# Attention streamed from HBM on one core: TensorE's program touches its far end first and ends with a wait for the last store, and the last V buffer is freed in two parts

## The chip, the core and the metric

The kernel runs on one core of a Trainium2 chip. The metric is device time in microseconds (us) of one execution; lower is better. All times of the trace are counted from the first instruction of the profiled execution.

## What is computed

```python
B, H, Sq, Skv, Dh = 8, 16, 16, 2048, 256          # q, k, v in bfloat16
scale = q.shape[-1] ** -0.5
scores = jnp.einsum('bhqd,bhkd->bhqk', q, k) * scale
attn = jax.nn.softmax(scores, axis=-1)
return jnp.einsum('bhqk,bhkd->bhqd', attn, v)
```

There are 128 heads, each with 16 queries and 2048 keys. K and V are 134 MB each, and every byte of them is read once, so the work is mostly a stream of two large tensors through the core.

## The kernel before

**Stages.** The 128 heads are worked off in 16 stages g = 0..15 of eight heads. A stage needs K and V of its eight heads, each in two halves of four heads; the code calls the half e = 0 or 1, and this document says K(g,a), K(g,b), V(g,a), V(g,b). A half is 4 MB: 128 partitions with 64 tokens (T) of 256 numbers each. `SL` has four buffers of that size, KA, KB, VA and VB. K of stage 0 goes into VA and VB; all later K goes into KA and KB, all V into VA and VB.

**SyncE** issues every load (`load`, L93, its DMA on L94) and the last store, in one fixed order (`on_sync`, L96): q, K(0,a), K(0,b), then for g = 1..15 K(g,a), K(g,b), V(g-1,a), V(g-1,b), and V(15,a), V(15,b) at the end. A load waits until the buffer that it overwrites has been read: K(g,e) waits for `c_qk[e]` (L103), which TensorE raises when it has used up K(g-1,e); V(w,e) waits for `c_pv[e]` (L115), raised when V(w-1,e) has been used up; V(0,e) waits for `c_qk[e]` of stage 0. SyncE waits at the head of its queue, so a load that waits holds back all loads behind it. Near the end loads are cut into pieces: K(15,a) and K(15,b) into two of 32 tokens, V(14,b) into 33 and 31 tokens, V(15,a) into 37 and 27 and V(15,b) into eight pieces from 19 down to 2 tokens (`PIECES`, L83, and `MID`, L85). Each piece has a semaphore of its own, so that TensorE can start on the first ones.

**VectorE** transposes each half of K in place in two instructions of 32 tokens each (L145), raising `c_kt[e][0]` and `c_kt[e][1]`. Later in the stage it takes the negative row maximum (L147), transposes the probabilities into `PTc` (L153) and inverts the row sums.

**ScalarE** prepares the scaled queries of the next stage (L165), takes the exponential (L191, raising `c_ex`), and spreads the transposed probabilities into the block pattern `PTz` by eight copies (L180, each raising `c_cp`): four for half a, after `c_pv[0]` says that half a of `PTz` is free, then the evacuation of the stage before (L173, raising `c_ev`) with its store, then four for half b.

**TensorE** (`on_tensor`) first runs QK for stage 0. Then follows a loop over r = 1..16 in TensorE's own program (a real loop with a branch back, not unrolled): QK of stage r (left out for r = 16), then PV of stage r-1. `qk` (L217, by way of `mm`) issues eight weight loads with one matmul of 128x512 for each bank c in `cs` behind each load (L212 is the matmul with a load, L213 those without). In the loop it is called four times, twice for each half, with two of the four banks at a time: banks 0 and 1 need only the first 32 tokens, so the first call waits for `c_kt[e][0]` and the second for `c_kt[e][1]`. QK for half a also waits for `c_ex[1]`, since it overwrites the scores of the stage before. PV is 64 matmuls of 128x256 for each half (L251), one for each token t, all into one bank; it waits for `c_ev`, for the copies (`c_cp`), for the V half (`s_v`) and in front of the first token of each piece for that piece (`s_p`).

**The end.** After PV of stage 15 ScalarE evacuates the result, SyncE stores it (L126, 64 KB) and waits for that store (`s_fin`, L127). TensorE's program ends when its loop ends, without a wait.

Of the kernel before, what the change touches and what calls it, by code (L numbers as in the profile page):

```python
# [4 lines left out]
ACTF = mybir.ActivationFunctionType  # L5
# [6 lines left out]
T = 64  # L12
# [3 lines left out]
def bass_standalone__softmax_full_bidir__sampling_kernel(  # L16
# [20 lines left out]
    with ExitStack() as es:  # L37
# [17 lines left out]
        def sem(name):  # L55
            return ec(nc.semaphore(name))
# [13 lines left out]
        c_ex = [sem("c_ex0"), sem("c_ex1")]  # L70
        c_pt = sem("c_pt")
        c_ri = sem("c_ri")
        c_cp = sem("c_cp")
        c_pv = [sem("c_pv0"), sem("c_pv1")]
        c_ev = sem("c_ev")

# [13 lines left out]
        def kslot(g, e):  # L90
            return (VA, VB)[e] if g == 0 else (KA, KB)[e]
# [4 lines left out]
        def on_sync(eng):  # L96
            eng.dma_start(QT[:], qh).then_inc(s_q, 16)  # L97
            for e in range(2):
                load(eng, ku, 0, e, kslot(0, e), 0, T, s_k0[e])
            for g in range(1, G):  # L100
                for e in range(2):
                    if g >= 2:
                        eng.wait_ge(c_qk[e], g)  # L103
                    if g < last:
                        load(eng, ku, g, e, kslot(g, e), 0, T, s_k[e])
                    else:
                        load(eng, ku, g, e, kslot(g, e), 0, 32, s_k[e])
                        load(eng, ku, g, e, kslot(g, e), 32, 32, s_kl[e])
                if g == 1:
                    for x in [c_ev] + list(s_p[0].values()) + list(s_p[1].values()):  # L110
                        eng.sem_inc(x, 1)
                for w in ((g - 1,) if g < last else (g - 1, g)):
                    for e in range(2):
                        if w:
                            eng.wait_ge(c_pv[e], w)  # L115
                        else:
                            eng.wait_ge(c_qk[e], 1)
                        pieces = [(0, T)]
                        if w == last:
                            pieces = PIECES[e]  # L120
                        elif (w, e) == (last - 1, 1):
                            pieces = [(0, MID), (MID, T - MID)]
                        for a, n in pieces:
                            load(eng, vu, w, e, (VA, VB)[e], a, n, s_p[e][a] if a else s_v[e])
            eng.wait_ge(c_ev, G + 1)
            eng.dma_start(oh[128 * last:128 * last + 128, :], O_fin[:, last, :]).then_inc(s_fin, 16)  # L126
            eng.wait_ge(s_fin, 16)  # L127
# [4 lines left out]
        def on_vector(eng):  # L132
            eng.memset(QW[:].rearrange("p e m x -> p (e m x)").bitcast(F32), 0.0).then_inc(c_qt, 1)  # L133
            eng.wait_ge(s_q, 16)
            qf = QT[:].bitcast(F32)
            eng.transpose(qf, qf).then_inc(c_qt, 1)  # L136
            for g in range(G):
                for e in range(2):
                    for h in range(2):
                        if h == 0:  # L140
                            eng.wait_ge(s_k[e] if g else s_k0[e], 16 * max(g, 1))
                        elif g == last:
                            eng.wait_ge(s_kl[e], 16)
                        x = SLf[:, kslot(g, e), 32 * h:32 * h + 32, :].rearrange("p t i -> p (t i)")
                        eng.transpose(x, x).then_inc(c_kt[e][h], 1)  # L145
                eng.wait_ge(c_qk[1], g + 1)
                eng.tensor_reduce(out=negm[:, g:g + 1], in_=S_ps[:].rearrange("p c n -> p (c n)"),  # L147
                                  axis=AX.X, op=ALU.max, negate=True).then_inc(c_mx, 1)
                for h in range(2):
                    eng.wait_ge(c_ex[h], g + 1)  # L150
                    if g and h == 0:
                        eng.wait_ge(c_cp, 8 * g)
                    eng.transpose(PTc[:, 32 * h:32 * h + 32, :].rearrange("p t x -> p (t x)"),  # L153
                                  P_sb[:, 1024 * h:1024 * h + 1024]).then_inc(c_pt, 1)
                eng.tensor_reduce(out=ltot[:, g:g + 1], in_=lsum[:, g, :], axis=AX.X, op=ALU.add).then_inc(c_ri, 1)  # L155
                eng.wait_ge(c_ri, 2 * g + 1)
                eng.reciprocal(rinv[:, g:g + 1], ltot[:, g:g + 1]).then_inc(c_ri, 1)  # L157

        def on_scalar(eng):
            def qwb(g):  # L160
                Q, r = g // 4, g % 4
                for a in range(4):
                    dv = QW[32 * a:32 * a + 32, 0, 16 * a, :]
                    sv = QT[32 * Q:32 * Q + 32, :]
                    eng.activation(ap_of(dv, dv.offset, [[1024 + 512, 2], [2, 64], [1, 2]]),  # L165
                                   ap_of(sv, sv.offset + 2 * (8 * r + a), [[8, 2], [64, 64], [1, 2]]),
                                   ACTF.Copy, scale=scale).then_inc(c_qw, 1)

            def evac(g):
                eng.wait_ge(c_pv[1], g + 1)  # L170
                if g == last:
                    eng.wait_ge(c_ri, 2 * G)
                eng.activation(O_fin[:, g, :], O_ps[:, 0:D], ACTF.Copy, scale=rinv[:, g:g + 1]).then_inc(c_ev, 1)  # L173

            def copies(e):
                for a in range(4):
                    rs = 32 * (2 * e + a // 2)
                    sv = PTc[rs:rs + 32, :, :]
                    m = 64 * e + 16 * a
                    eng.activation(PTz[32 * a:32 * a + 32, e, :, m:m + 16],  # L180
                                   sv[:, :, 16 * (a % 2):16 * (a % 2) + 16], ACTF.Copy).then_inc(c_cp, 1)

            eng.wait_ge(c_qt, 2)
            qwb(0)
            for g in range(G):
                if g < last:
                    eng.wait_ge(c_qk[1], g + 1)
                    qwb(g + 1)
                eng.wait_ge(c_mx, g + 1)
                for h in range(2):  # L190
                    eng.activation(P_sb[:, 1024 * h:1024 * h + 1024],  # L191
                                   S_ps[:, 2 * h:2 * h + 2, :].rearrange("p c n -> p (c n)"), ACTF.Exp,
                                   bias=negm[:, g:g + 1], scale=1.0, accum_out=lsum[:, g, h:h + 1]).then_inc(c_ex[h], 1)
# [12 lines left out]
            eng.wait_ge(s_st, 16 * last)  # L206

        def on_tensor(eng):
# [18 lines left out]
            eng.wait_ge(c_qw, 4)  # L227
            for e in range(2):
                eng.wait_ge(c_kt[e][1], 1)
                qk(e, (0, 1, 2, 3), kslot(0, e)).then_inc(c_qk[e], 1)  # L230

            with nc.Fori(1, G + 1, engines=[PE]) as r:
                with eng.If_lt(eng.to_reg(r), G):
                    for e in range(2):
                        for h in range(2):
                            eng.wait_ge(c_kt[e][h], r + 1)
                            if e == 0 and h == 0:
                                eng.wait_ge(c_ex[1], r)
                            ins = qk(e, (2 * h, 2 * h + 1), (KA, KB)[e])
                        ins.then_inc(c_qk[e], 1)  # L240
                lim1 = (r & 16) + 1
                lim2 = lim1 + ((r + 1) & 16)
                for e in range(2):
                    if e == 0:
                        eng.wait_ge(c_ev, r)
                    eng.wait_ge(c_cp, 8 * r - 4 + 4 * e)
                    eng.wait_ge(s_v[e], 16 * r)
                    for t in range(T):
                        if t in s_p[e]:
                            eng.wait_ge(s_p[e][t], lim2 if (e, t) == (1, MID) else lim1)  # L250
                        ins = eng.matmul(O_ps[:, 0:D], PTz[:, e, t, :], SL[:, (VA, VB)[e], t, :],  # L251
                                         start=(e == 0 and t == 0), stop=(e == 1 and t == T - 1))
                    ins.then_inc(c_pv[e], 1)

        on_sync(nc.sync)
        on_gpsimd(nc.gpsimd)
# [31 lines left out]
```

## Time and profile before

| | |
|---|---|
| three timed runs | 638.52, 637.37 and 638.66 us, median 638.52 |
| the profiled execution's own time | 637.77 us |
| its span, first to last instruction | 636.4 us |
| TensorE busy with matmuls, VectorE, ScalarE | 77%, 57%, 33% of the span |
| matmuls and weight loads | 3072 and 2544 |
| mean granted TensorE clock | 0.921 of full speed |
| bytes read by DMA | 269.48 MB |

The profiled execution's time is the span and 1.4 us around it. The profile's page has a row of 40 equal slices for each engine, in tenths of busy time; DMA in that row is the mean busy share of the 16 DMA engines, and the row below it is what they moved. "SPq" and "PEq" are the queues of SyncE and TensorE. A row of the timeline has the start, the length, the engine, the line and operation, how many such instructions were merged ("x2"), and in brackets the idle time ahead of it with what ended that. A row of the DMA issues ends with the time from issue to the last landing; a 4 MB load is one issue, and 16 DMA engines carry an equal part each.

### The profile page before, as it was taken

To read this page: it belongs to the slowest core of one execution; us is meant where nothing else is said; L and a number is where in the kernel's file an instruction comes from. 1 tells how busy PE (TensorE), PEld (TensorE's weight loads), DVE (VectorE), ACT (ScalarE), POOL (GpSimd) and SP (SyncE) were. 2 spreads that over 40 slices of the span, in tenths; PEclk is the share of its full clock that TensorE was granted. 3 is DMA by queue.
4 is the path that set the end of the run, shared out by engine and by line. 5 is a ranking of instruction groups with operands and counts; after the bars stand their busy time and mean duration, and the time that the engine had idled before them with its cause. 6 is when DMAs were issued, how large, how long until landed. Compare 5 with 4: busy or idle time off the path is not lost.

```text
span 636.4 us, 6411 instructions
## 1 busy us (share of the span) xinstructions
PE 489.3 (77%) x3072; PEld 271.0 (43%) x2544; DVE 361.7 (57%) x146; ACT 207.4 (33%) x273; POOL 7.1 (1%) x5
## 2 busy tenths in 40 slices
PE   0457999595995958879597895967959589597787
PEld 0002737154271533716336262452714428154376
DVE  2949683763738546294562935639366383766610
ACT  1024535225052250613416043160522505225050
POOL 4000000000000000000000000000000000000000
PEclk9997999798897989979799797998979899799999
DMA  8999999999999999999999999999999999999997
GB/s 371 445 437 420 413 432 430 431 432 434 433 430 432 431 431 432 439 432 430 430 431 428 432 432 431 435 431 432 428 432 435 430 433 437 426 427 425 431 395 288
DMA packets 13254, 270.60 MB, mean 425 GB/s; under 512 B 1472, under 2 KB 3776, under 8 KB 4416
## 3 DMA queue, kind: packets, MB, share of 16 engines
q1 hardware_dynamic: 11088, 269.55, 98.7%
q10 hardware_dynamic: 2160, 0.98, 0.5%
q8 instruction: 2, 0.03, 0.0%
q14 instruction: 4, 0.03, 0.0%
HBM read 269.48 MB, written 1.05 MB: 425 GB/s over the span
## 4 chain that ended last, share of the span: by engine, by line
DMA 63%; DVE 23%; PE 13%; ACT 0%; issue 0%; SPq 0%
DMA SL<-in_k_dram 56%; DVE SL L145 22%; DMA SL<-in_v_dram 7%; PE S_ps L213 5%; PE S_ps L212 5%; PE O_ps L251 4%; DVE PTc L153 0%; DVE negm L147 0%; ACT P_sb L191 0%; SPq L94 0%; ACT O_fin L173 0%; SPq L97 0%; DVE rinv L157 0%; DVE ltot L155 0%
## 5 line engine op out<-in xcount | busy, mean ns | idle before, releaser
L145 DVE STREAM_TRANSPOSE SL<-SL 128x4096 f32<-128x4096 f32 x64 | 280.8, 4424 | 154.8 <-DMA SL<-in_k_dram 154.8
L212 PE MATMUL S_ps<-SL,QW 128*128 128x512 bf16 x496 | 206.6, 417 | 140.3 <-DVE SL L145 140.2
L251 PE MATMUL O_ps<-SL,PTz 128*128 128x256 bf16 x2048 | 228.6, 273 | 3.4 <-DMA SL<-in_v_dram 3.2
L251 PEld LDWEIGHTS O_ps<-SL,PTz 128*128 128x128 bf16 x2048 | 198.4, 98 | 37.2 <-issue 7.5
L213 PE MATMUL S_ps<-SL,QW 128*128 128x512 bf16 x528 | 213.2, 414 | 0.0
L212 PEld LDWEIGHTS S_ps<-SL,QW 128*128 128x128 bf16 x496 | 72.6, 146 | 324.5 <-issue 177.7
L180 ACT ACTIVATE PTz<-PTc 32x1024 bf16<-32x1024 bf16 x128 | 134.9, 1054 | 48.3 <-PE O_ps L251 38.0
L165 ACT ACTIVATE QW<-QT 32x256 bf16<-32x256 bf16 x64 | 26.8, 419 | 297.8 <-PE S_ps L213 290.7
L147 DVE TENSOR_REDUCE negm<-S_ps 128x1 f32<-128x2048 f32 x16 | 36.7, 2292 | 64.9 <-PE S_ps L213 64.9
L153 DVE STREAM_TRANSPOSE PTc<-P_sb 128x1024 bf16<-128x1024 bf16 x32 | 37.9, 1224 | 20.3 <-ACT P_sb L191 20.3
L191 ACT ACTIVATE P_sb<-S_ps,negm 128x1024 bf16<-128x1024 f32 x32 | 35.4, 1110 | 26.5 <-DVE negm L147 26.5
L173 ACT ACTIVATE O_fin<-O_ps,rinv 128x256 bf16<-128x256 f32 x16 | 7.6, 474 | 52.8 <-PE O_ps L251 52.8
L130 POOL MEMSET PTz<- 128x8192 f32 x1 | 6.9, 6925 | 0.3 <-POOLq L273 0.3
L191 ACT ACTIVATION_READ_ACCUMULATOR P_sb<-S_ps,negm 128x1 f32 x32 | 6.3, 196 | 0.0
L136 DVE STREAM_TRANSPOSE QT<-QT 128x2048 f32<-128x2048 f32 x1 | 2.3, 2311 | 3.7 <-DMA QT<-in_q_dram 3.7
L157 DVE RECIPROCAL rinv<-ltot 128x1 f32<-128x1 f32 x16 | 2.6, 164 | 0.5
L155 DVE TENSOR_REDUCE ltot<-lsum 128x1 f32<-128x2 f32 x16 | 1.8, 113 | 0.0
L165 ACT ACT_TABLE_LOAD x1 | 1.3, 1283 | 0.7 <-PEq L273 0.7
L133 DVE MEMSET QW<- 128x1024 f32 x1 | 0.9, 912 | 1.0 <-PEq L273 1.0
L273 POOL MEMSET const-bfloat16-1.0<- 128x1 bf16 x1 | 0.1, 103 | 0.0
L273 POOL MEMSET const-uint8-127<- 128x1 uint8 x1 | 0.1, 103 | 0.0
L273 POOL MEMSET const-float32-0.0<- 128x1 f32 x1 | 0.1, 100 | 0.2 <-issue 0.2
(1 smaller groups left out, 0.1 us busy)
## 6 DMA issues: line engine op xcount, KB each, us to landing
SL<-in_k_dram SPq DMA_DIRECT2D x30, 4096.0 KB, 25.8
SL<-in_v_dram SPq DMA_DIRECT2D x29, 4096.0 KB, 29.1
SL<-in_k_dram SPq DMA_DIRECT2D x4, 2048.0 KB, 23.0
SL<-in_v_dram SPq DMA_DIRECT2D x1, 2368.0 KB, 8.6
SL<-in_v_dram SPq DMA_DIRECT2D x1, 2112.0 KB, 27.2
SL<-in_v_dram SPq DMA_DIRECT2D x1, 1984.0 KB, 31.5
SL<-in_v_dram SPq DMA_DIRECT2D x1, 1728.0 KB, 12.5
SL<-in_v_dram SPq DMA_DIRECT2D x1, 1216.0 KB, 8.9
```

The costliest lines, as they stand in the source:

```text
L130: eng.memset(PTz[:].rearrange("p a t c -> p (a t c)").bitcast(F32), 0.0).then_inc(c_pool, 1)
L145: eng.transpose(x, x).then_inc(c_kt[e][h], 1)
L147: eng.tensor_reduce(out=negm[:, g:g + 1], in_=S_ps[:].rearrange("p c n -> p (c n)"), axis=AX.X, op=ALU.max, negate=True).then_inc(c_mx, 1)
L153: eng.transpose(PTc[:, 32 * h:32 * h + 32, :].rearrange("p t x -> p (t x)"), P_sb[:, 1024 * h:1024 * h + 1024]).then_inc(c_pt, 1)
L157: eng.reciprocal(rinv[:, g:g + 1], ltot[:, g:g + 1]).then_inc(c_ri, 1)
L165: eng.activation(ap_of(dv, dv.offset, [[1024 + 512, 2], [2, 64], [1, 2]]), ap_of(sv, sv.offset + 2 * (8 * r + a), [[8, 2], [64, 64], [1, 2]]),
L173: eng.activation(O_fin[:, g, :], O_ps[:, 0:D], ACTF.Copy, scale=rinv[:, g:g + 1]).then_inc(c_ev, 1)
L180: eng.activation(PTz[32 * a:32 * a + 32, e, :, m:m + 16], sv[:, :, 16 * (a % 2):16 * (a % 2) + 16], ACTF.Copy).then_inc(c_cp, 1)
L191: eng.activation(P_sb[:, 1024 * h:1024 * h + 1024], S_ps[:, 2 * h:2 * h + 2, :].rearrange("p c n -> p (c n)"), ACTF.Exp, bias=negm[:, g:g ...
L212: return eng.matmul(dst, w, x, start=start, stop=stop)
L213: return eng.add_instruction(mybir.InstMatmult(name=nc.get_next_instruction_name(), engine=PE, start_tensor_calc=start, stop_tensor_calc=stop,
L251: ins = eng.matmul(O_ps[:, 0:D], PTz[:, e, t, :], SL[:, (VA, VB)[e], t, :], start=(e == 0 and t == 0), stop=(e == 1 and t == T - 1))
```

## The change

- TensorE's program is put into named blocks. It starts with a branch to a block "far", which stands behind the loop's end and does nothing but branch back to "near", the program proper. After the loop TensorE branches to "over", behind "far".
- In "over" TensorE waits for the last store (`s_fin`), as SyncE does.
- PV of half a raises a new semaphore `c_pm` after token 36. SyncE issues the first 37 tokens of V(15,a) after `c_pm` of the 15th pass, and the other 27 after `c_pv[0]`, as before.
- In the loop, QK for half a is one call with all four banks (one weight load for four matmuls, eight loads instead of 16), and waits for the whole transposed half, `c_kt[0][1]`. Half b stays at two calls.
- `c_cp` becomes two semaphores, one for each half of `PTz`; VectorE waits for both.
- The limits for the waits are computed into registers at other places of the loop.

```diff
-        c_cp = sem("c_cp")
+        c_cp = [sem("c_cp0"), sem("c_cp1")]
+        c_pm = sem("c_pm")
...
                         if w:
-                            eng.wait_ge(c_pv[e], w)
+                            eng.wait_ge(c_pm if (w, e) == (last, 0) else c_pv[e], w)
...
                         for a, n in pieces:
+                            if (w, e, a) == (last, 0, PIECES[0][1][0]):
+                                eng.wait_ge(c_pv[0], w)
                             load(eng, vu, w, e, (VA, VB)[e], a, n, s_p[e][a] if a else s_v[e])
...
                     if g and h == 0:
-                        eng.wait_ge(c_cp, 8 * g)
+                        for x in c_cp:
+                            eng.wait_ge(x, 4 * g)
...
-            with nc.Fori(1, G + 1, engines=[PE]) as r:
-                with eng.If_lt(eng.to_reg(r), G):
+            nc.br("far", engines=[PE])
+            with nc.body("near", valid_engines=[PE]):
...
+                with nc.Fori(1, G + 1, engines=[PE]) as r:
+                    rr = eng.to_reg(r)
+                    r4, r16, lim1 = eng.to_reg(4 * r), eng.to_reg(16 * r), eng.to_reg((r & 16) + 1)
+                    with eng.If_lt(rr, G):
+                        for e in range(2):
+                            for cs in (((0, 1, 2, 3),), ((0, 1), (2, 3)))[e]:
+                                eng.wait_ge(c_kt[e][cs[-1] // 2], r + 1)
+                                if e == 0:
+                                    eng.wait_ge(c_ex[1], rr)
+                                ins = qk(e, cs, (KA, KB)[e])
+                            ins.then_inc(c_qk[e], 1)
                     for e in range(2):
-                        for h in range(2):
-                            eng.wait_ge(c_kt[e][h], r + 1)
-                            if e == 0 and h == 0:
-                                eng.wait_ge(c_ex[1], r)
-                            ins = qk(e, (2 * h, 2 * h + 1), (KA, KB)[e])
-                        ins.then_inc(c_qk[e], 1)
...
+                        for t in range(T):
...
+                            if (e, t + 1) == (0, PIECES[0][1][0]):
+                                ins.then_inc(c_pm, 1)
+                        ins.then_inc(c_pv[e], 1)
+                        if e == 0:
+                            lim2 = eng.to_reg((r & 16) + ((r + 1) & 16) + 1)
+                nc.br("over", engines=[PE])
+            with nc.body("far", valid_engines=[PE]):
+                eng.nop()
+                nc.br("near", engines=[PE])
+            nc.switch_bb("over")
+
+            eng.wait_ge(s_fin, 16)
```

More of the change, by code (lines that the diff above doesn't have):

```diff
@@ L180, in copies @@
                     eng.activation(PTz[32 * a:32 * a + 32, e, :, m:m + 16],
[L181 removed]
+                                   sv[:, :, 16 * (a % 2):16 * (a % 2) + 16], ACTF.Copy).then_inc(c_cp[e], 1)
             eng.wait_ge(c_qt, 2)
@@ L225, in qk @@
                 return ins
[L227 to L230, printed above, removed]
-            with nc.Fori(1, G + 1, engines=[PE]) as r:
-                with eng.If_lt(eng.to_reg(r), G):
-                    for e in range(2):
-                        for h in range(2):
-                            eng.wait_ge(c_kt[e][h], r + 1)
-                            if e == 0 and h == 0:
-                                eng.wait_ge(c_ex[1], r)
-                            ins = qk(e, (2 * h, 2 * h + 1), (KA, KB)[e])
-                        ins.then_inc(c_qk[e], 1)
[L241 to L253, printed above, removed]
@@ new lines, in on_tensor @@
+            nc.br("far", engines=[PE])
+            with nc.body("near", valid_engines=[PE]):
+                eng.wait_ge(c_qw, 4)
+                for e in range(2):
+                    eng.wait_ge(c_kt[e][1], 1)
+                    qk(e, (0, 1, 2, 3), kslot(0, e)).then_inc(c_qk[e], 1)
+                with nc.Fori(1, G + 1, engines=[PE]) as r:
+                    rr = eng.to_reg(r)
+                    r4, r16, lim1 = eng.to_reg(4 * r), eng.to_reg(16 * r), eng.to_reg((r & 16) + 1)
+                    with eng.If_lt(rr, G):
+                        for e in range(2):
+                            for cs in (((0, 1, 2, 3),), ((0, 1), (2, 3)))[e]:
[4 more added lines that the diff above has]
+                            ins.then_inc(c_qk[e], 1)
+                    for e in range(2):
+                        if e == 0:
+                            eng.wait_ge(c_ev, rr)
+                        eng.wait_ge(c_cp[e], r4)
+                        eng.wait_ge(s_v[e], r16)
+                        for t in range(T):
+                            if t in s_p[e]:
+                                eng.wait_ge(s_p[e][t], lim2 if (e, t) == (1, MID) else lim1)
+                            ins = eng.matmul(O_ps[:, 0:D], PTz[:, e, t, :], SL[:, (VA, VB)[e], t, :],
+                                             start=(e == 0 and t == 0), stop=(e == 1 and t == T - 1))
+                            if (e, t + 1) == (0, PIECES[0][1][0]):
+                                ins.then_inc(c_pm, 1)
+                        ins.then_inc(c_pv[e], 1)
+                        if e == 0:
+                            lim2 = eng.to_reg((r & 16) + ((r + 1) & 16) + 1)
+                nc.br("over", engines=[PE])
```

## The prediction, made before the changed kernel was run

> **What bounds the kernel now.** I read the page's span, slices and chain first.
>
> ```profile
> span 636.4 us, 6411 instructions
> DMA  8999999999999999999999999999999999999997
> HBM read 269.48 MB, written 1.05 MB: 425 GB/s over the span
> DMA 63%; DVE 23%; PE 13%; ACT 0%; issue 0%; SPq 0%
> ```
>
> The DMA engines are full in every slice but the first and the last. The chain's DVE and PE parts are work that releases loads while earlier loads still run. So the end moves only by time in which the DMA engines are left without work, and by what follows the last landing. In the middle a late issue costs nothing:
>
> ```profile
> SL<-in_k_dram SPq DMA_DIRECT2D x30, 4096.0 KB, 25.8
> SL<-in_v_dram SPq DMA_DIRECT2D x29, 4096.0 KB, 29.1
> ```
>
> A K half lands 25.8 us after its issue. Its own transfer takes 9.7 us: in the rows below V(0,a) lands at 33.05 + 21.1 = 54.2 and V(0,b) at 41.09 + 22.8 = 63.9. So it stood behind other loads for some 16 us. I then looked for the places without such cover, by landing times and the windows, and found two, and a third thing behind the last landing.
>
> **Place 1, the load of K(2,a).** Timeline and DMA issues, stages 0 and 1:
>
> ```profile
> 24.22 0.62 PE L212 MATMUL S_ps<-SL,QW 128*128 128x512 bf16 x1 [24.22 <-DVE SL L145]
> 33.05 0.33 SPq L94 DMA_DIRECT2D SL<-in_v_dram  x1
> 41.09 0.33 SPq L94 DMA_DIRECT2D SL<-in_v_dram  x1
> 47.18 8.75 DVE L145 STREAM_TRANSPOSE SL<-SL 128x4096 f32<-128x4096 f32 x2
> 51.66 0.65 PE L212 MATMUL S_ps<-SL,QW 128*128 128x512 bf16 x1 [10.61 <-DVE SL L145]
> 60.49 8.25 SPq L94 DMA_DIRECT2D SL<-in_k_dram  x2
> ...
> SL<-in_v_dram SPq DMA_DIRECT2D x1, 4096.0 KB, 21.1
> SL<-in_v_dram SPq DMA_DIRECT2D x1, 4096.0 KB, 22.8
> SL<-in_k_dram SPq DMA_DIRECT2D x1, 4096.0 KB, 15.1
> 68.42 16.84 DMA SL<-in_k_dram
> ```
>
> K(2,a) is issued at 60.49, when QK(1,a) has ended, only 3.4 us ahead of V(0,b)'s landing at 63.9, and everything behind it in SyncE's queue waits too. It lands at 75.6, 11.7 us after V(0,b) where 9.7 would do: 2.0 us are lost already. K(2,b) follows at 85.3, 9.7 later, and from there on the queue is deep.
>
> **Place 2, the load of V(15,a).**
>
> ```profile
> 580.15 0.80 SPq L94 DMA_DIRECT2D SL<-in_v_dram  x2
> 602.32 7.17 PE O_ps L251 x64
> 609.51 0.33 SPq L94
> 616.50 0.47 ACT L173 ACTIVATE O_fin<-O_ps,rinv 128x256 bf16<-128x256 f32 x1 [2.63 <-PE O_ps L251]
> ...
> SL<-in_v_dram SPq DMA_DIRECT2D x1, 1984.0 KB, 31.5
> SL<-in_v_dram SPq DMA_DIRECT2D x1, 2368.0 KB, 8.6
> 609.00:610.00 1.00, 1.00 (x12) 0.90 (x10) 0.00 (x0) 0.43 (x1) 0.00 (x0) 1.00 0.63 270
> 610.00:611.00 1.00, 1.00 (x12) 0.90 (x10) 0.00 (x0) 0.98 (x2) 0.00 (x0) 1.00 1.39 370
> 611.00:612.00 1.00, 1.00 (x12) 0.90 (x10) 0.00 (x0) 0.98 (x2) 0.00 (x0) 1.00 0.44 152
> 612.00:616.00 4.00, 4.00 (x39) 3.59 (x38) 0.00 (x0) 1.84 (x2) 0.00 (x0) 1.00 1.03 433
> ```
>
> V(15,a) is issued at 609.51, when PV(14,a) has ended; the last piece of V(14,b), the second issue behind 580.15, lands 31.5 us after it, at 612.0. The last column, GB/s, falls to 270, 370 and 152 in three windows and is 433 afterwards: (270 + 370 + 152)/433 = 1.8 of 3 us were used, 1.2 lost. By the last landings it is less: the first piece (37 of 64 tokens, 5.6 us of transfer) lands at 618.1, 6.1 after 612.0: 0.5 lost.
>
> **The end.**
>
> ```profile
> q8 instruction: 2, 0.03, 0.0%
> ...
> q8 instruction: 1, 0.02, 5.8%
> ...
> DMA packets 145, 0.08 MB, mean 33 GB/s; under 512 B 16, under 2 KB 144, under 8 KB 144
> q8 instruction: 1, 0.02, 3.4%
> ...
> q1 hardware_dynamic: 9, 0.00, 2.7%
> ...
> 633.59 0.35 SPq L126 DMA_DIRECT2D out_dram<-O_fin  x1
> SPq L127 <- DMA out_dram<-O_fin: 2.5, 1, 2.5
> ```
>
> In the window 634.0 to 636.45 one packet of the instruction queue ran for 3.4% of 16 engines' 2.45 us, 1.3 us, beside the 144 packets of the last store. In the window 635.2 to 636.45 nine of those 144 are left, one engine's sixteenth. So fifteen engines were done by 635.2, and one, behind the code fetch, at the span's end, 636.4: the fetch holds the store up by 1.2 us. The other packet of this queue (the second row, window 68 to 69) ran when TensorE entered the second part of its loop for the first time; I take the queue for TensorE's.
>
> **The change part by part**, against the profiled execution's own 637.77 us (span 636.4 and 1.4 around it); the median shown, 638.52, is 0.75 above it.
>
> *QK for half a in one call.* 15 x 8 = 120 weight loads go. They lie beside matmuls: stage 0, with one load for four matmuls, takes 24.22 to 33.05 = 8.83 us for 32, stage 1, with one for two, 51.66 to 60.49 = 8.83. Worth nothing. But QK(1,a) now starts when both transposes are done, 47.18 + 8.75 = 55.93, not at 51.66, and takes at least the same 8.83 us. K(2,a) is then issued at 64.8 or later, after V(0,b) has landed. How much later hangs on the granted clock, the column ahead of the last two:
>
> ```profile
> 51.60:54.90 3.30, 3.24 (x8) 0.79 (x5) 3.30 (x2) 3.23 (x4) 0.00 (x0) 0.50 1.06 457
> 158.00:164.10 6.10, 6.02 (x15) 1.27 (x8) 5.00 (x3) 0.00 (x0) 0.00 (x0) 0.50 1.02 437
> ```
>
> After an idle stretch QK starts at half the clock, here for 3.3 us in stage 1 and for 6.1 in a later one. At half clock a matmul takes 3.3/8 = 0.41 us, at full 0.22, so each further us costs half a us: up to 1.4. K(2,a) is issued at 64.8 to 66.2. An empty queue starts with a delay: V(15,a)'s first piece landed 8.6 us after its issue for 5.6 of transfer, 3.0 on top. K(2,a) lands at 64.8 + 3.0 + 9.7 = 77.5 to 78.9 instead of 75.6: +2.0 to +3.4. I take the middle, **+2.7**. From the other side: the engines' mean rather than the last landing could put it at 4.0; the start of the kernel, where q is issued at 0.74 and K(0,b) has landed at 25.0 with 2.4 + 2 x 9.7 us of transfer, had a delay of 2.4 and would give +1.3. Nothing behind it can give that back, as the queue is full until place 2.
>
> In stages 2 to 14 the same delay, 4 to 5 us at QK(g,a) and less at PV, lies inside the 16 us of cover: nothing. Without that cover it would cost 4 us a stage. In stage 15 K(15,a)'s second transpose releases QK at 587.15; 64 matmuls at 0.22 end at 601.2, and V(14,a) lands at 602.3: 1.1 us of room, which a half clock would use up. The rows, with those of the start and the end:
>
> ```profile
> 587.15 0.44 PE L212 MATMUL S_ps<-SL,QW 128*128 128x512 bf16 x1 [1.16 <-DVE SL L145]
> ...
> 573.01 29.26 DMA SL<-in_v_dram
> ...
> 633.09 0.47 ACT O_fin L173
> ...
> 0.74 0.38 SPq L97
> 1.65 23.35 DMA SL<-in_k_dram
> ```
>
> *The last V in two parts.* `c_pm` rises after 37 of PV(14,a)'s 64 matmuls, 602.32 + 37 x 0.11 = 606.4, 3.1 us ahead of 609.51. SyncE has nothing else between; the second piece follows at 609.5 as before, and V(15,b), behind it, waits for 616.5 anyway. 5.6 us of lead should nearly close the gap; place 1 lost some with 3.4. Gain 0.5 to 1.2, taken **-0.9**. TensorE is next: PV(15) is 128 matmuls at 7.17/64 = 0.11 us, 14.3 in all, and can start at 617.0, when the evacuation of stage 14 is done, ending at 631.3. The evacuation after it now starts at 633.09, so 1.8 us of room are left.
>
> *The far branch and the end wait.* The branch out and back runs while TensorE idles up to 24.22. It moves the fetch near 69 us to the start, where it delays one of 16 engines; place 1 levels that: nothing. [...] The store then lands at 635.2: **-1.2**, bounds 0 and -1.3.
>
> [...]
>
> *The rest.* `c_cp` in two semaphores: the copies run in order on ScalarE, so the same copies release the same waits. The register work is a few instructions beside 7 us of matmuls. Nothing.
>
> **The sum**: 637.8 + 2.7 - 0.9 - 1.2 = **638.4 us**, 0.1 under the median.
>
> **Rivals.**
> 1. *The start is hidden* (faster). If the queue of V(0,b) is deeper than I read, or the half clock shorter, K(2,a) costs at most 1 us: 637.8 + 0.7 - 0.9 - 1.2 = 636.4. For it: the rows show one execution. Against: 64.8 is after 63.9.
> 2. *The long clock* (slower). 6.1 us of half clock at QK(1,a), and half clock again at QK(15,a), which takes the gain of place 2: 637.8 + 3.4 + 0 - 1.2 = 640.0. It decides once the stretch in stage 1 passes 5 us. For it: other stages show it. Against: by the delay above TensorE idles only some 4 us ahead of QK(15,a), against 10.6 ahead of QK(1,a).
> [...]
> 4. *The wait does not keep the fetch away*: 637.8 + 2.7 - 0.9 = 639.6, within the bound.
>
> **How the numbers follow.** A measurement tells about 0.2%, 1.3 us, from no change. Forecast 0.40 and rival 4 0.08 lie within it: 0.48 the same. Rival 1 has 0.22: faster. Rivals 2 and 3 have 0.12 and 0.18: slower 0.30. The range has to take in most of rivals 1 and 3: 636.2 to 640.8; the forecast's own is 637.2 to 639.6.
>
> **What would show it.** K(2,a) issued at 65 to 66 and landing at 77.5 to 79, GB/s near zero in a window ahead of it: step one. V(15,a)'s first piece issued 5 to 6 us ahead of V(14,b)'s last landing, and no window under 400 GB/s there: step two. No instruction packet beside the last store, all its packets landed within 1.6 us of the issue, and the span ending there: step three. The forecast is wrong if K(2,a) lands at 76, or if the time around the span grows by the fetch.

## The result

The changed kernel is slower: 641.58 us in the median of five runs (640.84 to 641.72), beside 638.47 for the kernel before on the same chip (five runs, 637.13 to 638.66). The ratio is 1.0052, with a 95% interval of 1.0037 to 1.0067. That is above the forecast of 638.4 and above the range's upper end of 640.8. The profiled execution took 641.72 us, 3.95 more than that of before: its span is 640.0 instead of 636.4, and around the span lie 1.7 us instead of 1.4.

The page of the changed kernel, its span, slices, instruction queue, traffic and the share of the chain (in the numbering of its own lines, L148 is the K transpose, L216 and L217 are QK, L258 is PV, L95 the loads):

```profile
span 640.0 us, 6279 instructions
DMA  8999899999999999999999999999999999999997
GB/s 372 442 430 395 328 428 430 436 443 432 430 426 432 429 433 440 436 430 426 427 431 432 432 442 435 428 426 430 426 433 441 440 430 426 430 424 427 433 419 280
q8 instruction: 1, 0.02, 0.0%
HBM read 269.48 MB, written 1.05 MB: 423 GB/s over the span
DMA 48%; PE 28%; DVE 23%; ACT 0%; issue 0%; SPq 0%
```

The slices show where to look. All of them are as full as before except the fifth, 64 to 80 us, with 328 GB/s, and a little less in the one ahead of it. This is place 1.

**Place 1.** The timeline of the changed kernel, stages 0 and 1, and K(2,a)'s issue row (the last column is the time from issue to landing):

```profile
16.83 4.45 DVE L148 STREAM_TRANSPOSE SL<-SL 128x4096 f32<-128x4096 f32 x1 [7.40 <-DMA SL<-in_k_dram]
25.75 0.62 PE L216 MATMUL S_ps<-SL,QW 128*128 128x512 bf16 x1 [25.75 <-DVE SL L148]
48.71 17.40 DVE L148 STREAM_TRANSPOSE SL<-SL 128x4096 f32<-128x4096 f32 x4
57.52 0.65 PE L216 MATMUL S_ps<-SL,QW 128*128 128x512 bf16 x1 [14.93 <-DVE SL L148]
66.56 0.33 SPq L95 DMA_DIRECT2D SL<-in_k_dram  x1
...
SL<-in_k_dram SPq DMA_DIRECT2D x1, 4096.0 KB, 12.1
```

QK(1,a) starts at 57.52 behind two transposes, 48.71 + 8.8, as the prediction said, but everything here is 1.5 us later than it reckoned: QK(0) starts at 25.75 and not at 24.22. K(2,a) is issued at 66.56 and lands at 78.7. The windows of the changed kernel (columns as in the prediction, the last is GB/s), and behind them two of before:

```profile
62.00:63.00 1.00, 1.00 (x6) 0.15 (x1) 1.00 (x1) 0.00 (x0) 0.00 (x0) 1.00 0.76 328
63.00:64.00 1.00, 1.00 (x7) 0.14 (x1) 1.00 (x1) 0.00 (x0) 0.00 (x0) 1.00 0.08 33
64.00:65.00 1.00, 1.00 (x6) 0.14 (x1) 1.00 (x1) 0.00 (x0) 0.00 (x0) 1.00 0.00 0
65.00:66.00 1.00, 1.00 (x7) 0.14 (x1) 1.00 (x1) 0.00 (x0) 0.00 (x0) 1.00 0.00 0
66.00:67.00 1.00, 1.00 (x6) 0.28 (x2) 0.12 (x1) 0.00 (x0) 0.00 (x0) 1.00 0.00 0
67.00:68.00 1.00, 1.00 (x6) 0.37 (x3) 0.00 (x0) 0.00 (x0) 0.00 (x0) 1.00 1.84 492
```

```profile
63.00:64.00 1.00, 1.00 (x5) 0.14 (x1) 1.00 (x1) 0.00 (x0) 0.00 (x0) 1.00 1.08 361
64.00:65.00 1.00, 0.42 (x3) 0.22 (x2) 0.58 (x1) 0.00 (x0) 0.00 (x0) 1.00 1.05 360
```

From 63 to 67 us the DMA engines of the changed kernel move almost nothing: four microseconds in which the stream that sets the time stands still. Before, the same place shows two windows of 360.

**Place 2.** The changed kernel around the last V (the rows of QK(15) are in the first two lines, with the granted clock ahead of the last two columns):

```profile
590.40:597.20 6.80, 5.75 (x14) 0.63 (x4) 5.75 (x3) 1.12 (x2) 0.00 (x0) 0.50 1.04 443
597.20:604.00 6.80, 6.80 (x33) 1.60 (x11) 4.12 (x1) 0.00 (x0) 0.00 (x0) 1.00 1.03 443
616.00:622.00 6.00, 6.00 (x58) 5.38 (x56) 0.00 (x0) 3.77 (x4) 0.00 (x0) 1.00 0.96 411
622.00:625.00 3.00, 2.43 (x24) 1.94 (x22) 0.00 (x0) 2.08 (x3) 0.00 (x0) 1.00 0.95 358
625.00:626.00 1.00, 1.00 (x12) 0.90 (x10) 0.00 (x0) 0.97 (x2) 0.00 (x0) 1.00 0.68 236
626.00:627.00 1.00, 1.00 (x12) 0.90 (x10) 0.00 (x0) 0.97 (x2) 0.00 (x0) 1.00 1.01 374
627.00:628.00 1.00, 1.00 (x12) 0.89 (x10) 0.00 (x0) 0.66 (x1) 0.00 (x0) 1.00 0.91 370
```

The gap ahead of V(15,a) is closed (411 GB/s from 616 to 622), but a new one stands behind it: against 415 GB/s the windows from 622 to 628 lose (3 x 57 + 179 + 41 + 45)/415 = 1.05 us. V(15,b) waits for the end of PV(14), and PV(14) is late: TensorE idled for 5.1 us ahead of QK(15) and then ran at half clock for 6.8 us, so that PV(14) starts at 608.3, 1.7 us after V(14,a) has landed (606.6). What the early piece of V(15,a) gained went back there.

**The end.** The store in the changed kernel:

```profile
637.90 0.47 ACT L177 ACTIVATE O_fin<-O_ps,rinv 128x256 bf16<-128x256 f32 x1 [10.24 <-PE O_ps L258]
638.40 0.35 SPq L129 DMA_DIRECT2D out_dram<-O_fin  x1
...
out_dram<-O_fin SPq DMA_DIRECT2D x1, 64.0 KB, 1.5
```

No instruction packet, and 1.5 us instead of 2.8. The evacuation starts 4.8 us later than before (637.90 against 633.09), the store gives 1.3 back, and 0.3 to 0.4 come behind the span: 4.8 - 1.3 + 0.4 = 3.9, the difference of the two profiled executions.

### The profile page after: what moved, and what is told of

Read it like the earlier page. It is cut to its first block, busy times and chain, and to the rows that moved or that the text cites. A ratio compares the mean times of both kernels' runs of the same rounds, so it can differ in the third digit from the quotient of the medians.

```text
span 640.0 us, 6279 instructions
## 1 busy us (share of the span) xinstructions
PE 483.0 (75%) x3072; PEld 254.3 (40%) x2424; DVE 361.6 (57%) x146; ACT 207.4 (32%) x273; POOL 7.1 (1%) x5
## 3 DMA queue, kind: packets, MB, share of 16 engines
HBM read 269.48 MB, written 1.05 MB: 423 GB/s over the span
## 4 chain that ended last, share of the span: by engine, by line
DMA 48%; PE 28%; DVE 23%; ACT 0%; issue 0%; SPq 0%
DMA SL<-in_k_dram 47%; DVE SL L148 21%; PE S_ps L217 17%; PE S_ps L216 7%; PE O_ps L258 3%; DMA SL<-in_v_dram 1%; DVE PTc L157 1%; DVE negm L150 1%; ACT P_sb L195 0%; SPq L95 0%; ACT O_fin L177 0%; SPq L98 0%; DVE rinv L161 0%; DVE ltot L159 0%
## 5 line engine op out<-in xcount | busy, mean ns | idle before, releaser
L148 DVE STREAM_TRANSPOSE SL<-SL 128x4096 f32<-128x4096 f32 x64 | 280.8, 4424 | 121.1 <-DMA SL<-in_k_dram 121.1
L216 PE MATMUL S_ps<-SL,QW 128*128 128x512 bf16 x376 | 152.8, 406 | 154.1 <-DVE SL L148 154.0
L258 PE MATMUL O_ps<-SL,PTz 128*128 128x256 bf16 x2048 | 226.7, 273 | 0.8 <-ACT O_fin L177 0.6
L217 PE MATMUL S_ps<-SL,QW 128*128 128x512 bf16 x648 | 226.5, 421 | 0.0
L258 PEld LDWEIGHTS O_ps<-SL,PTz 128*128 128x128 bf16 x2048 | 199.5, 98 | 31.3 <-issue 4.9
L216 PEld LDWEIGHTS S_ps<-SL,QW 128*128 128x128 bf16 x376 | 54.7, 146 | 352.0 <-issue 217.5
```

Source lines behind the costliest of these rows:

```text
L216: return eng.matmul(dst, w, x, start=start, stop=stop)
L217: return eng.add_instruction(mybir.InstMatmult(name=nc.get_next_instruction_name(), engine=PE, start_tensor_calc=start, stop_tensor_calc=stop,
```

## The experiments

The theory from these two traces: place 1 is the loss. The merged call starts QK(1,a) late, and the far branch, which the prediction costed at nothing, makes it later. The rivals: the far branch alone; the late QK in every stage; something at the end. Each kernel ran beside the kernel before on the same chip, whose median was 637.02 in the first group, 636.89 in the second and 636.90 in the third, so ratios are compared, not times.

| kernel | median us | ratio to before, 95% interval |
|---|---|---|
| the whole change (five runs with the prediction) | 641.58 | 1.0052 [1.0037, 1.0067] |
| e1 changed, without the far branch | 640.15 | 1.0048 [1.0029, 1.0067] |
| e2 changed, QK half a in two calls | 636.93 | 1.0000 [0.9989, 1.0010] |
| e3 before, merged call alone | 641.52 | 1.0069 [1.0050, 1.0088] |
| e4 before, end wait alone | 637.45 | 1.0006 [0.9994, 1.0017] |
| e5 before, V(15,a) in two parts alone | 636.54 | 0.9988 [0.9976, 1.0000] |
| e6 before, far branch alone | 638.17 | 1.0009 [0.9997, 1.0020] |
| e7 before, two parts and end wait | 636.62 | 0.9995 [0.9984, 1.0006] |
| e9 changed, K(1,a) transposed early | 635.77 | 0.9979 [0.9969, 0.9989] |
| e8 before, two parts, end wait, K(1,a) half early | 635.87 | 0.9982 [0.9971, 0.9994] |
| e10 before, two parts, K(1,a) early | 635.46 | 0.9981 [0.9971, 0.9990] |
| e11 the whole change again | 640.79 | 1.0061 [1.0047, 1.0075] |
| e12 as e1, beside e11 | 639.87 | 1.0048 [1.0031, 1.0064] |

### The merged call: e3, e2

e3 is the kernel before with QK of half a in one call:

```diff
-                        for h in range(2):
-                            eng.wait_ge(c_kt[e][h], r + 1)
-                            if e == 0 and h == 0:
+                        for cs in (((0, 1, 2, 3),), ((0, 1), (2, 3)))[e]:
+                            eng.wait_ge(c_kt[e][cs[-1] // 2], r + 1)
+                            if e == 0:
                                 eng.wait_ge(c_ex[1], r)
-                            ins = qk(e, (2 * h, 2 * h + 1), (KA, KB)[e])
+                            ins = qk(e, cs, (KA, KB)[e])
```

> The kernel before with one edit: QK of half a in one call that waits for both transposes. Theory: QK(1,a) starts at 55.9, K(2,a) is issued at 64.8 to 66.2 and lands at 77.5 to 79; time 640.5 to 642.0, as slow as the whole change, since the store still ends behind the fetch. Rival, the merged call is hidden: 637.5 to 638.7.

It took 641.52 us, ratio 1.0069: this edit alone is at least as slow as the whole change. Place 1 of e3, timeline, issue row and windows:

```profile
56.19 0.65 PE L212 MATMUL S_ps<-SL,QW 128*128 128x512 bf16 x1 [14.93 <-DVE SL L145]
65.44 0.33 SPq L94 DMA_DIRECT2D SL<-in_k_dram  x1
...
SL<-in_k_dram SPq DMA_DIRECT2D x1, 4096.0 KB, 13.4
...
64.00:65.00 1.00, 1.00 (x6) 0.14 (x1) 0.78 (x1) 0.00 (x0) 0.00 (x0) 1.00 0.00 0
65.00:66.00 1.00, 1.00 (x6) 0.38 (x3) 0.00 (x0) 0.00 (x0) 0.00 (x0) 1.00 0.00 0
```

K(2,a) is issued at 65.4 and lands at 78.8, in the expected bounds. It also shows the second cost of the merged call. PV(14) starts at 607.36 and V(15,a) is issued at 614.54, 5.0 us later than before, where place 1 explains 3.3: QK(15) ran at half clock from 589.5 to 596.2 (0.50 in that window), and in this kernel V(15,a) waits for all of PV(14,a). In landings, K(2,a) comes 3.3 us later than before (78.8 against 75.6), and so does the last piece of V(14,b) (615.3 against 612.0); the first piece of V(15,a) comes 4.9 later (614.54 + 8.5 = 623.0 against 618.1). So in this execution some 3.3 us were lost at place 1 and 1.6 at place 2.

e2 is the changed kernel with the call split again:

```diff
-                            for cs in (((0, 1, 2, 3),), ((0, 1), (2, 3)))[e]:
+                            for cs in ((0, 1), (2, 3)):
```

> The changed kernel with QK of half a in two calls again, as half b has it (eight weight loads more in the loop). Theory: QK(1,a) starts with the first transposed 32 tokens near 53.1, K(2,a) is issued at 62 to 63.5 and lands at 75 to 77; QK(15) is done before V(14,a) lands, so the early part of V(15,a) keeps its gain; time 636.3 to 638.0. Rival, the merged call costs nothing and the branch at the start is the loss: K(2,a) is late all the same and the time stays above 640. Also told: whether the wait for the store still keeps the code fetch away from it when the program is eight instructions longer.

636.93, ratio 1.0000: undoing this one edit takes the whole loss away, K(2,a) is issued at 61.95, and there is no gain left over, though both edits that were to gain are in. Both halves of the pair say the same, so the merged call as the main cause is shown, not only argued.

### Is it place 1, or the late QK of every stage: e9

e9 is the whole change, and VectorE transposes both parts of K(1,a) before the softmax of stage 0; K(1,a) has landed by then and VectorE is idle:

```diff
+            EARLY = [(1, 0, 0), (1, 0, 1)]
...
             for g in range(G):
                 for e in range(2):
                     for h in range(2):
+                        if (g, e, h) not in EARLY:
+                            kt(g, e, h)
+                if g == 0:
+                    for x in EARLY:
+                        kt(*x)
```

(`kt` holds the wait and the transpose that stood in the loop.)

> The whole change, and VectorE transposes K(1,a), which landed at 35 us, before the softmax of stage 0 instead of behind it. Nothing else moves, the merged call and the far branch stay. Theory, place 1 is the bulk of the loss: QK(1,a) starts near 48 to 50 instead of 57.5, K(2,a) is issued at 57 to 60 and lands at 74 to 76 instead of 78.7; 3.5 to 4.3 us under the changed kernel, ratio to the kernel before 0.998 to 1.001. Rival, the late QK of every stage and the fetch are the loss: ratio 1.003 or more.

635.77, ratio 0.9979: with the merged call in all 15 stages, the far branch and the end wait still in, the kernel is faster than before. Its rows at place 1, the transpose, the issue and two windows:

```profile
35.91 8.77 DVE L148 STREAM_TRANSPOSE SL<-SL 128x4096 f32<-128x4096 f32 x2 [0.94 <-DMA SL<-in_k_dram]
58.12 0.33 SPq L95 DMA_DIRECT2D SL<-in_k_dram  x1
...
63.00:64.00 1.00, 1.00 (x6) 0.40 (x3) 0.00 (x0) 0.00 (x0) 0.00 (x0) 1.00 1.07 459
64.00:65.00 1.00, 1.00 (x7) 0.29 (x4) 0.00 (x0) 0.00 (x0) 0.00 (x0) 1.00 1.22 524
```

K(2,a) is issued some 7 us before V(0,b) has landed (42.26 + 22.8 = 65.1), and nothing is lost. From 1.0052 to 1.0061 for the change to 0.9979 is some 0.8%, 5 us, by one move on an engine that is idle there, and more than the 3.5 to 4.3 us that were expected, since place 1 now loses less than in the kernel before. Place 1 is the cause. The late QK of stages 2 to 14 costs nothing that can be told, as predicted: e10 below, with K(1,a) early and without the merged call, the branch and the wait, has 0.9981.

### The far branch: e1, e12 beside e11, e6

e1 and e12 are the changed kernel without the two branches:

```diff
-            nc.br("far", engines=[PE])
-            with nc.body("near", valid_engines=[PE]):
...
-                nc.br("over", engines=[PE])
-            with nc.body("far", valid_engines=[PE]):
-                eng.nop()
-                nc.br("near", engines=[PE])
-            nc.switch_bb("over")
```

> The changed kernel without the branch to the far end and back; all else kept, the wait for the last store too. Theory: the branch fetches a block of code at 2.3 us on one DMA engine, so q and the first K halves land 1.5 us late on that engine, and the issue of K(2,a), which has no cover, comes 1.5 us late. Without it K(2,a) is issued at 65.0 to 66.4 instead of 66.6 and lands at 77.5 to 79; the fetch comes back near 69 us; time 640.0 to 641.0. Rival, the fetch at the start is the whole loss: K(2,a) lands by 76 and the time is 638 or less.

1.0048: most of the loss stays, so the rival of the far branch alone falls. K(2,a) was issued at 64.75 and landed at 78.2. Since the other chip's kernel before is 1.4 us quicker, the pair was repeated on one chip:

> The changed kernel once more, on the same chip as the next one, which differs by the far branch alone. If the far branch costs through place 1: K(2,a) is issued 1.2 to 1.8 us later than without it, and the time is 1 to 2 us longer. If it costs nothing in the time: within 0.4 us.

> The changed kernel without the far branch, beside the one above. If the far branch costs through place 1: 1 to 2 us under it. If not: within 0.4 us.

640.79 with the branch (spans 638.5 to 639.5), 639.87 without (637.7 to 639.3): 0.9 between the medians, 0.65 between the means, and the spans overlap. The direction is that of the theory, the size is about half of what was expected, and six runs each do not fix it. K(2,a) is issued at 66.45 with the branch and at 66.04 without, 0.4 later and not the expected 1.2 to 1.8. The branch does make QK(1,a) start 1.1 us later (57.18 against 56.04), but in e12 the half clock of QK(1,a) lasts some 5.8 us, in e11 4.3, and in e1, the same kernel as e12, 3.1. Rows of e1 and of e12:

```profile
56.10:59.10 3.00, 3.00 (x8) 0.29 (x3) 3.00 (x1) 0.00 (x0) 0.00 (x0) 0.50 0.99 426
59.20:62.00 2.80, 2.80 (x15) 0.46 (x4) 2.80 (x2) 0.00 (x0) 0.00 (x0) 1.00 0.89 386
```

```profile
56.10:61.70 5.60, 5.60 (x14) 0.57 (x4) 5.60 (x2) 0.00 (x0) 0.00 (x0) 0.50 0.92 398
61.90:63.00 1.10, 1.10 (x6) 0.15 (x1) 1.10 (x1) 0.00 (x0) 0.00 (x0) 1.00 1.11 477
```

So one kernel issues K(2,a) 1.3 us earlier or later from execution to execution (64.75 and 66.04), by the length of the half clock, (5.8 - 3.1)/2 = 1.35, and that covers most of what the branch does. The start of the changed kernel shows where the branch's part comes from: DMA issue rows of q and the window from 2 to 4 us.

```profile
QT<-in_q_dram SPq DMA_DIRECT2D x1, 1024.0 KB, 6.4
...
q8 instruction: 1, 0.02, 4.4%
```

The row of q in the kernel before:

```profile
QT<-in_q_dram SPq DMA_DIRECT2D x1, 1024.0 KB, 4.9
```

The code fetch, one packet of 16 KB, runs 4.4% of 16 engines' 2 us, 1.4 us, beside the loads of q and K(0,a). q then lands 6.4 us after its issue, where the page of before has 4.9. Of the 16 landings of q in that trace 15 lie between 5.3 and 5.6 us and one at 7.1, and of K(0,a)'s 15 between 15.0 and 15.4 and one at 16.8; before, all 16 of q lie between 5.1 and 5.6 and all of K(0,a) between 14.8 and 15.3. The transpose of K(0,a) starts at the last landing in both, and all that hangs on it comes 1.5 us later (16.83 against 15.31). Without the branch (e1 and e12) q lands 5.0 and 4.9 us after its issue again, and QK(0) starts at 24.32 and 24.28 instead of 25.75.

e6 is the kernel before with the branch out and back alone, its lines the ones that e1 takes out:

> The kernel before with one edit: TensorE's program first branches to its far end and back; there is no wait at the end. Theory: the fetch at the start makes one DMA engine 1.5 us late, QK(0) and QK(1) start 1.2 to 1.5 us later, K(2,a) is issued near 62 instead of 60.5 and the late engine stays late to the end: slower by 0.7 to 1.5 us, ratio 1.001 to 1.0025; the fetch near 69 us is gone. Rival, the fetch at the start is levelled by place 1, as the prediction had it: ratio 0.9995 to 1.0005, or below where the fetch beside the last store goes too.

1.0009 with an interval from 0.9997 to 1.0020: between what the theory (1.001 to 1.0025) and its rival (0.9995 to 1.0005) expected, and not clear of nothing. K(2,a) was issued at 61.82, and there was no fetch beside the last store (window 635.2 to 637). There were two fetches at the start (4.6% of 16 engines in the window from 1.5 to 4 us, 5.6% from 8.9 to 10), where the changed kernel has one (4.4% from 2 to 4); TensorE's program in e6 has eight weight loads more.

### The last V in two parts: e5

```diff
+                            if (w, e, a) == (last, 0, PIECES[0][1][0]):
+                                eng.wait_ge(c_pv[0], w)
...
+                        if (e, t + 1) == (0, PIECES[0][1][0]):
+                            ins.then_inc(c_pm, 1)
```

> The kernel before with one edit: the first 37 tokens of V(15,a) are freed by their own semaphore. Theory: QK(15) and PV(14) are on time when the call is not merged, so the first piece is issued near 606.4 and DMA has no gap at 609 to 612; the gain of about 1 us stays, since V(15,b) is issued at 616.5 ahead of V(15,a)'s landing at 620 to 621. The store still ends behind the code fetch. Time 0.6 to 1.3 us under the kernel before, a ratio of 0.998 to 0.999. Rival, V(15,b) runs dry instead, as in the changed kernel: ratio 0.9995 to 1.0005.

0.9988: 0.8 us under the kernel before by the ratio, with an interval that ends at none, beside the 0.9 of the prediction. The trace agrees: the windows from 609 to 612 and from 612 to 616 show 422 and 420 GB/s, where the kernel before falls to 270, 370 and 152. So this part closes the gap, as it was said to do; its size is not fixed by the interval.

### The end wait and the store: e4, e7, e13, e14

e4 adds the wait behind the loop of the kernel before; e7 adds it and the two parts.

```diff
                     ins.then_inc(c_pv[e], 1)
+
+            eng.wait_ge(s_fin, 16)
```

> The kernel before with one edit: TensorE ends with the wait for the last store. Theory: no code fetch beside the last store, which takes 1.6 us from issue to landing instead of 2.8; 1.2 less span, of which 0.3 may come back behind the span: 636.2 to 637.6. [...]

> The kernel before with the two edits that the prediction counted as gains and without the two that cost: V(15,a) in two parts and TensorE's wait for the last store, no far branch, no merged call. Theory: DMA ends 1.0 us earlier, the store takes 1.6 us instead of 2.8, and 0.3 us come back behind the span: 1.5 to 2.0 us under the kernel before, ratio 0.997 to 0.9977. Rival, the store's gain is not there in most runs of the kernel before: ratio 0.998 to 0.999.

1.0006 and 0.9995: no gain that can be told, and e7 falls short even of its rival's 0.998 to 0.999. In the traces of both the store takes 1.5 us and stands alone. But the spans of the timed runs are hardly shorter (medians 635.45 for e4 and 635.7 for its kernel before; 634.95 for e7 and 635.1 for e5), and the time around the span is 1.6 to 1.7 us in the median instead of 1.3 in every kernel that ends with this wait. So either the store is not held up in most executions of the kernel before, or something gives it back. Two more profiled executions of the kernel before, e13 and e14, tell:

> The kernel before, one more look at its trace. If the code fetch stands beside the last store in every execution: one instruction packet behind 633 us and a store of 2.3 to 2.9 us from issue to its last landing. If only in some: no such packet here or in the next look, and a store of 1.6 us.

> The kernel before, a further look for the same question: an instruction packet beside the last store and a store of 2.3 us or more, or none and 1.6 us.

Store and last window of e13 (the kernel before), then of e5 (whose TensorE program ends in the same way):

```profile
DMA packets 144, 0.07 MB, mean 26 GB/s; under 512 B 16, under 2 KB 144, under 8 KB 144
q1 hardware_dynamic: 144, 0.07, 9.1%
out_dram<-O_fin SPq DMA_DIRECT2D x1, 64.0 KB, 1.5
```

```profile
q1 hardware_dynamic: 144, 0.07, 9.8%
q8 instruction: 1, 0.02, 2.4%
out_dram<-O_fin SPq DMA_DIRECT2D x1, 64.0 KB, 2.2
```

No fetch in e13, and e14 issues its store at 634.96 and its span ends at 636.5, 1.5 us later as well (636.62 and 637.85 us, one run each). Of five profiled executions in which TensorE's program is as long as that of before and ends without the wait, two show the fetch beside the store (before 2.8 us for it, e5 2.2), two show none (e10 and e13, each 1.5), and e14 has the same 1.5. For e10 that is against its expectation below. The prediction's 1.2 us was read from an execution that happened to have it. Why some have it and others do not stays open.

### Versions that beat both: e8, e10

e8 is e7 with the first 32 tokens of K(1,a) transposed early; e10 is e5 with both parts early, without the wait. The edit is that of e9:

```diff
+            EARLY = [(1, 0, 0)]                  # e8
+            EARLY = [(1, 0, 0), (1, 0, 1)]       # e10
```

> The kernel before with V(15,a) in two parts, TensorE's wait for the last store, and the first 32 tokens of K(1,a) transposed before the softmax of stage 0; no far branch, no merged call. Theory: K(2,a) is issued near 55 to 57, lands 9.7 us after V(0,b), and place 1 loses nothing: 0.8 to 2 us under the same kernel without the early transpose, ratio to the kernel before 0.9965 to 0.998. Rival, nothing is left to gain at place 1: ratio 0.9985 to 0.9995.

> The same without the wait for the last store, and with both parts of K(1,a) transposed early. Theory: as fast as the one with the wait or up to 0.5 us faster, since the wait's gain in the span has not shown in the timed runs and the wait costs 0.3 us behind the span; a code fetch stands beside the last store. Rival, the store's gain is real in the time: 0.5 to 1 us slower than with the wait.

0.9982 and 0.9981, 635.87 and 635.46 us, both faster than the kernel before and than the change; e8 is just short of the 0.9965 to 0.998 that were expected, and between the two nothing can be told by the ratio. K(2,a) is issued at 55.7 and 57.6 and in e10 the windows from 63 to 66 and from 609 to 616 show 377 to 524 GB/s. e9's 0.9979 is no better in what can be told, and it carries three edits that are not needed.

## Why the prediction was wrong, point by point

The sum was 638.4 us, and the profiled execution took 641.7. By the sum the last evacuation comes 2.7 - 0.9 = 1.8 us later than before; it came 4.8 later. These 3.0 us are the miss, and 0.3 more came behind the span. Two steps failed there. The far branch was put at nothing and made place 1 worse: some four us lost, not 2.7. And the gain of 0.9 at V(15,a) was taken as kept, with 1.1 us of room for QK(15) that the half clock used up. The rest of the 3.0, under 1 us, is not placed. A third step, the end wait, held in the two profiled executions but is no gain of the kernel.

- **QK for half a in one call**: the mechanism was right and the place too, and so, nearly, was the size at place 1. K(2,a) lands at 78.7, within the forecast's 77.5 to 78.9. Without the far branch it lands at 78.8, 78.2 and 79.6 (e3, e1, e12), 2.7 to 4.1 us after the 75.6 of before, beside the prediction's 2.0 to 3.4. One landing is no exact measure: in e13 and e14, two executions of the kernel before, K(2,a) is issued at 61.1 and 61.2 and lands at 75.8 and 77.0. The windows of the whole change lose about four microseconds more than those of before, where the landing moved by only 3.1. In the kernel before, the landing was one late engine's: 15 of K(2,a)'s 16 landings lie between 73.4 and 74.9 us and one at 75.55, and the code fetch, from 68.8 to 69.7, ran during this very load. In the changed kernel all 16 lie between 78.15 and 78.7, and its only fetch is at 2.3. What the time followed is the stretch in which all engines stand still (the four windows from 63 to 67 us with 33, 0, 0 and 0 GB/s), which the prediction named "the engines' mean" and set aside. The empty queue's delay was 12.1 - 9.7 = 2.4 (2.7 in e11) and not 3.0. What the term put at nothing is stage 15: in e3, where V(15,a) is freed in one part, the merged call cost 1.6 us more at place 2.
- **The far branch**: "place 1 levels that: nothing" is a step that failed. It looked at the late engine's bytes, which place 1 does level (V(0,b)'s last landing at 65.4 is 1.4 us behind the other 15, K(2,a)'s at 78.7 is level with them), and not at who waits for the late engine: q, K(0,a), QK(0), QK(1) and K(2,a), which has no cover. QK(1,a) starts at 57.52 and 57.18 with the branch, at 56.08 and 56.04 without; K(2,a) is issued at 66.56 and 66.45 with it, at 64.75 and 66.04 without. Some 0.9 us by the medians of e11 and e12, 0.6 by the ratio of e6, not closely fixed.
- **Stages 2 to 14**: right, shown by e9 beside e10.
- **Weight loads, `c_cp` in two, register work**: at nothing. e9 carries them all and is faster than before, so none of them can cost much; none was tried alone.
- **The last V in two parts**: -0.9 agrees with this part alone (e5, -0.8 with an interval to nothing). In the whole change the half clock at QK(15), which the prediction gave 1.1 us of room and put into rival 2, came (6.8 us of it in the profiled execution) and the gain went back at V(15,b). That the half clock is the whole reason is not shown: e5, without it, has 382 GB/s from 616 to 622, and e9, with 6.8 us of it, has 378 and 376 from 617 to 620 and from 620 to 623; each is about half of the changed kernel's loss. In the second profiled execution of the change, e11, the half clock lasted 3.4 us and the windows show 408 and 422 GB/s at the same place, so there the gain stayed.

```profile
590.50:593.90 3.40, 2.97 (x7) 0.31 (x2) 2.90 (x2) 0.84 (x1) 0.00 (x0) 0.50 0.97 413
622.00:625.00 3.00, 3.00 (x30) 2.70 (x28) 0.00 (x0) 2.92 (x4) 0.00 (x0) 1.00 0.97 408
625.00:628.00 3.00, 3.00 (x29) 2.56 (x27) 0.00 (x0) 0.79 (x1) 0.00 (x0) 1.00 1.02 422
```

- **The end wait**: -1.2 is about what the stores of the two profiled executions differ by (1.5 against 2.8), and not what the kernel gains: e4 and e7 show none, and the wait costs 0.3 us behind the span. The step that failed is taking one execution's store for every execution's. No run shows that the wait is what keeps the fetch from the store, on which the -1.2 rests: e10 and e13 have a store of 1.5 us and no fetch without the wait, e4 and e7 do not gain with it. The 0.18 of rival 3 was the author's estimate; the changed kernel's one instruction packet is at 2.3 us, and what happens behind the span is not in the traces.
- **Rivals**: rival 2 comes nearest, in kind: the half clock in stage 15. Against it the prediction had TensorE idle for only some 4 us ahead of QK(15,a); it idled for 5.1 (e11 4.8, e1 3.7, and the half clock came there too). In stage 1 of the changed kernel the half clock lasted from 57.5 to 61.3, so rival 2's own point, a stretch over 5 us, was not reached; in e12 it was.

## What to carry to other kernels

In a kernel that streams at full DMA rate, look for the one load whose issue comes just in time, and cost every edit upstream of it at its full delay; elsewhere the same delay was free here, behind some 16 us of other loads (e9 0.9979, with the late call in all stages, beside e10's 0.9981). The last stage, where that cover ends, needs its own sum (1.6 us at place 2 in e3). Measure a stall of the stream by the windows in which the DMA engines move nothing (four us at place 1), not by the last landing of one load, which moved by only 3.1 there, since one engine was late in the kernel before. And before a term is read from a single event at the end of one trace, take a second execution: the store of the kernel before took 2.8 us in one and 1.5 in the next.

## What the runs showed of the hardware

- **The code fetch at the end comes and goes**: of three executions of the kernel before, one has it (2.8 us for the store) and two have a store of 1.5 us. With e5 and e10, whose TensorE programs are as long, it is two with (2.2 and 2.8 us) and three of 1.5.
- **Eight weight loads more, one fetch more.** In the changed kernel the far branch goes with one fetch at the start (16 KB, from 2.3 to 3.7 us), in e6, whose TensorE program holds eight weight loads more, with two (4.6% of 16 engines in the window from 1.5 to 4 us, 5.6% from 8.9 to 10). The kernel before has two in its whole span, at 68.8 and 634.1 us, and the changed kernel that one, so the 16 passes of the loop brought no further ones in these two executions. What sets a fetch off is not shown.
- **Half clock after a short idle.** In e4 TensorE idled only from about 616.2 to 618.7 while it waited for V(15,a), and PV(15) still began at half clock. The evacuation then started 1.3 us after the last landing, where e3 has 0.5:

```profile
615.00:618.40 3.40, 1.20 (x11) 0.83 (x9) 0.00 (x0) 1.72 (x3) 0.00 (x0) 1.00 0.97 413
618.40:621.80 3.40, 3.10 (x15) 2.23 (x16) 0.00 (x0) 2.96 (x3) 0.00 (x0) 0.50 0.99 413
```

The first window has matmuls in 1.20 of its 3.4 us, and the clock is halved right behind it. e6 shows the same (0.50 from 619.2 to 622.5, behind 2.1 us of idle time). PV(15) takes 15.65 us in e4 and 15.81 in e6. In before, e13, e14 and e3, where the same idle time was 1.6 to 1.8 us, it takes 14.8 to 14.9. So it does in the kernels that free V(15,a) early (14.4 to 14.9): TensorE is idle for 0.6 us there in the changed kernel and for 1.3 in e5. So that edit may have a second use, which the prediction did not see.
